# Centroid products of the later pairs moved in front of the odd cycles' products with v

## The chip, the cores and the metric

The kernel runs on one core of one Trainium2 chip. The metric is the device time of one execution in microseconds (us). The kernel before takes 772.41 us (median of three runs, 772.18 to 772.73). About 0.2% (1.5 us) is what a measurement of this kernel can tell from no change.

## The reference, cut to what matters

Clustered attention (2 batches, 8 heads, 768 rows, head width 64, 16 centroids per head) is followed by two dense blocks on 1536 x 512 tokens. The dense blocks are not touched.

```
q_assign = argmax(q_n @ c_n.T)          # nearest centroid of each query row
k_assign = argmax(k_n @ c_n.T)          # nearest centroid of each key row
scores = where(q_assign == k_assign, q @ k.T / 8, -1e9)
attn = exp(scores - max) / (sum + 1e-9)
out = attn @ v
x = out (heads side by side); x = moe(x); return moe2(x)
```

## The kernel before, in words

The attention works on 8 pairs (batch, two heads) numbered 0 to 7. A pair's queries and keys are turned by TensorE, split into a high and a low part (`th`, `tl`), and stacked by DMAs on SP's queue into two tiles per head, `st` for queries and `st` for keys; one-hot rows of the assigned centroids are stacked under them, so that one product gives scores and mask.

**Cycles.** The scores of one head are 12 blocks of 128 rows, worked off in two halves of 6. There are 16 heads, so 16 *cycles* d = 0 to 15. In a cycle, `run_cycle` reads a string of words, left to right, and each word issues its instructions on all engines; every engine runs its own instructions in exactly that order (the kernel is in a manual schedule). The words:

- `S5` to `S10`: the scores of a block (four matmuls, lines 582 and 585, into one of two `s` buffers of PSUM), then on VectorE the negated row maximum `nm` (line 591). Blocks are numbered from the cycle's own first; S6 to S10 belong to the next cycle.
- `E5` to `E10`: on ScalarE the exponential of a block into `p` with its row sum (line 600). It also frees the `s` buffer: S9 uses that of S7, and so waits for E7.
- `T0` to `T11`, `t0` to `t11`: three transposes of `p` blocks by TensorE into one of three `pt` buffers of PSUM (line 637; the same three buffers serve every preparatory transpose and product named below), and the copy to SBUF, by ScalarE for `T` (line 642), by VectorE for `t` (line 640). The fourth in a row waits until the first is copied out.
- `V`: the product of the cycle's transposed blocks with v (line 651), 24 matmul records of tiles 64 columns wide.
- `P`: the next step of preparing a later pair. A pair has 12 steps: `q0`, `q1`, `k0`, `k1` (turn a half of the queries or keys, line 497, ScalarE's copy at line 503, GpSimd's split at lines 479 and 480; `k1` also loads a later pair); `dt` (the products with the centroids, line 518, 8 matmul records of tiles 32 columns wide, then ScalarE's copy `dc`, line 521); `pd` (`dc` turned back, line 525); `max/ge` (VectorE, lines 534 and 535); a multiplication on GpSimd (line 537); `stack0` (five DMAs of head 0, line 475); a maximum (line 543); a comparison (line 545); `po` (load of the next v, three transposes at line 553, ScalarE's `oht` at line 555, four DMAs of one-hot rows of head 0).
- `K`: the stacking of the pair's second head, first the five DMAs, at the second K its four one-hot DMAs.
- `R`: the reciprocal of the row sums on VectorE, GpSimd's `line`, a DMA `flat`. `B`: its spreading back by two DMAs. `X`, `Y`: the scaled result and its split. `W`, `w`: one step of a weight conversion, most of them on VectorE.

Pair i is prepared from the end of cycle 2i-4 to the middle of cycle 2i-2; its first scores are S6 of cycle 2i-1. Cycle 0 has a string of its own (BEGIN), cycles 1 to 12 use ODD and EVEN in turn, and cycles 13 to 15 have strings of their own. Pair 1's `dt` stands in the opening part, those of pairs 2 to 7 in ODD.

```
scores_of(n): scores(n, 0); scores(n, 1); row_max(n)
"P": next(made, None)
"K": second.pop(0)(1)
```

Of the kernel before, what the change touches and what calls it, by code (L numbers as in the profile page):

```python
# [19 lines left out]
P = 128  # L20
# [13 lines left out]
def attention_moe_moe(  # L34
# [19 lines left out]
    B, H, S, D = q.shape  # L54
# [150 lines left out]
    with ExitStack() as actx:  # L205
# [483 lines left out]
        def run_cycle(d, order):  # L689


            for word in order.split():
                what, arg = word[0], int(word[1:] or 0)
                n = NJ * d + arg
                if what == "S":
                    if n < NJ * NDBL:
                        scores_of(n)
                elif what == "E":
                    if n < NJ * NDBL:
                        row_exp(n)  # L700
                elif what in "Tt":
                    p_transpose(2 * d + arg // NJ, arg % NJ, what == "t")
                    next_slot()
                elif what == "P":
                    next(made, None)
                elif what == "R":
                    inverse(d)
                elif what == "V":
                    p_v(d)
                elif what == "X":  # L710
                    if opsum:
                        x_rows(min(opsum))
                elif what == "K":
                    if second:
                        second.pop(0)(1)
                elif what == "B":
                    spread()
                elif what == "Y":
                    if x32s:
                        x_parts()  # L720
                elif what in "Ww":
                    pump(1 if d >= FIRST + (what == "w") else 0)
                elif what == "N":
                    next_slot()
            if d == 3:
                issue_chunk(0)

        PRE = ""
        BEGIN = "S3 P T0 T1 S4 E3 P T2 E4 P T3 S5 E5 t4 T5 S6 T6 T7 E6 P R S7 t8 T9 E7 T10 P B S8 P E8 P K S9 K P t11 S10 V E9 E10"
        EVEN = "P S5 T0 T1 P t2 E5 S6 T3 P T4 E6 t5 S7 R T6 P T7 E7 K S8 X T8 T9 E8 Y t10 B K S9 P w P E9 t11 S10 W E10 V"  # L730
        ODD = "S5 T0 T1 P t2 S6 E5 T3 T4 t5 S7 E6 P T6 R E7 T7 X S8 Y P E8 t8 T9 S9 T10 B P t11 E9 W S10 V P P E10 W"
        LATE_ODD = "S5 T0 T1 t2 E5 S6 T3 R T4 t5 S7 X Y E6 T6 T7 E7 S8 E8 t8 T9 S9 T10 B t11 S10 E9 V W W W E10"
        LATE_EVEN = "S5 T0 t1 t2 E5 S6 T3 T4 E6 R T5 S7 X Y E7 T6 S8 T7 t8 W S9 E8 t9 B T10 E9 t11 W S10 W V E10"
        LAST = "S5 T0 E5 t1 T2 T3 X t4 R t5 Y t6 T7 t8 B T9 t10 T11 W V W W W X Y"
# [1 line left out]
        for d in range(-1, NDBL):  # L736
            run_cycle(d, PRE if d < 0 else BEGIN if d == 0 else
                      {13: LATE_ODD, 14: LATE_EVEN, 15: LAST}.get(d, (EVEN, ODD)[d % 2]))
        manual.close()
# [145 lines left out]
```

## Time and profile before

| | |
|---|---|
| median of the runs | 772.41 us |
| profiled execution, its own time | 772.37 us |
| its span (first to last instruction) | 770.6 us |
| TensorE busy | 761.0 us (99%) |
| VectorE, ScalarE, GpSimd busy | 568.6, 360.9, 255.0 us |
| attention, with cycles 0 to 15 | about the first 245 us |

The span is the time on the core; the execution's own time has 1.8 us around it. In the profile PE is TensorE's matmul, DVE is VectorE, ACT ScalarE, POOL GpSimd, SPq the DMA queue of SyncE. A matmul's end is modelled, so PE counts as busy over small gaps; the starts tell more.

### The profile page before, as it was taken

The page shows a single profiled execution, that of the slowest core. Times are in us where ns is not written, and L with a number is a line of the kernel's source. Part 1 is how long each engine was busy: PE and PEld are TensorE (multiplying, and loading weights), DVE is VectorE, ACT ScalarE, POOL GpSimd, SP SyncE. Part 2 cuts the span into 40 slices and gives each one's busy share as a digit, 9 for nine tenths or more (in the row PEclk, how much of TensorE's full clock was granted, in tenths as well). Part 3 has the DMA queues.
Part 4 walks back from the last instruction along what each step waited for, and adds up shares of the span by engine and source line. Part 5 has one row for each costly group of instructions (what it writes and reads, how often), then busy time and mean ns, then how long its engine had stood idle before and what let it go on. Part 6 is the DMA issues. An engine that isn't in the chain of part 4 may idle for free.

```text
span 770.6 us, 10609 instructions
## 1 busy us (share of the span) xinstructions
PE 761.0 (99%) x3888; PEld 606.6 (79%) x3889; DVE 568.6 (74%) x824; ACT 360.9 (47%) x672; POOL 255.0 (33%) x390
## 2 busy tenths in 40 slices
PE   8999999999999999999999999999999999999998
PEld 5677777777776888888888888888888888888886
DVE  6676588797888868787798787888867787555552
ACT  6777676777574544534334343333534222222220
POOL 6347458566544412222221133422222211111110
PEclk9999999999999999999999999999999999999999
DMA  8865767665532123113131121021121111000012
GB/s 203 213 156 132 196 144 189 154 172 131 132 99 68 54 108 100 64 56 110 54 110 56 55 98 67 4 106 56 55 105 60 54 56 56 0 1 1 27 42 95
DMA packets 49667, 70.10 MB, mean 91 GB/s; under 512 B 28592, under 2 KB 33936, under 8 KB 49616
## 3 DMA queue, kind: packets, MB, share of 16 engines
q1 hardware_dynamic: 49328, 69.27, 31.6%
q8 instruction: 30, 0.49, 0.3%
q10 hardware_dynamic: 288, 0.16, 0.1%
q14 instruction: 21, 0.17, 0.1%
HBM read 46.17 MB, written 3.19 MB: 64 GB/s over the span
## 4 chain that ended last, share of the span: by engine, by line
PE 84%; DVE 4%; DMA 4%; ACT 3%; POOL 2%; issue 1%; SPq 1%; DVEq 0%; ACTq 0%; POOLq 0%
PE h L790 11%; PE h L788 11%; PE y L790 11%; PE h L789 11%; PE y L789 11%; PE y L788 11%; PE o L651 6%; PE pt L637 3%; PE s L582 3%; PE s L585 2%; ACT p L600 2%; DVE nm L591 2%; DMA st<-tl 1%; ACT p_t L642 1%; DMA st<-t 1%
## 5 line engine op out<-in xcount | busy, mean ns | idle before, releaser
L750 POOL TENSOR_SCALAR gh<-g 128x512 fp32r<-128x512 f32 x96 | 71.1, 741 | 290.1 <-DVE g L781 165.0
L788 PE MATMUL h<-xh,w 128*128 128x512 f32 x384 | 149.5, 389 | 0.2 <-ACT p L600 0.2
L790 PE MATMUL h<-xh,w 128*128 128x512 f32 x384 | 149.6, 390 | 0.0
L789 PE MATMUL h<-xl,w 128*128 128x512 f32 x384 | 149.5, 389 | 0.0
L591 DVE TENSOR_REDUCE nm<-s 128x1 f32<-128x768 f32 x96 | 91.5, 953 | 42.2 <-PE s L585 39.8
L600 ACT ACTIVATE p<-s,nm 128x768 f32<-128x768 f32 x96 | 87.5, 911 | 20.3 <-DVE nm L591 19.0
L777 ACT ACTIVATE p<-h,ones 128x512 f32<-128x512 f32 x48 | 33.0, 689 | 134.1 <-DVE m L776 133.7
L754 DVE TENSOR_TENSOR gl<-g,gh 128x512 fp32r<-128x512 f32 x96 | 72.1, 751 | 22.3 <-POOL gh L750 16.1
L790 PEld LDWEIGHTS h<-xh,w 128*128 128x128 f32 x384 | 72.1, 188 | 15.5 <-issue 0.6
L788 PEld LDWEIGHTS h<-xh,w 128*128 128x128 f32 x384 | 72.1, 188 | 15.2 <-issue 0.4
L789 PEld LDWEIGHTS h<-xl,w 128*128 128x128 f32 x384 | 72.1, 188 | 15.0
L637 PE MATMUL pt<-ident,p 128*128 128x128 f32 x576 | 81.2, 274 | 1.5 <-ACT p L600 0.6
L642 ACT ACTIVATE p_t<-pt 128x384 f32<-128x384 f32 x126 | 57.4, 491 | 40.8 <-PE pt L637 39.9
L582 PE MATMUL s<-st,st 128*128 128x384 f32 x192 | 73.7, 384 | 2.1 <-ACT p L600 0.8
L637 PEld LDWEIGHTS pt<-ident,p 128*128 128x128 f32 x576 | 66.9, 140 | 11.2 <-ACT p L600 4.9
L788 PE MATMUL y<-gh,w 128*128 128x512 f32 x192 | 74.7, 389 | 0.0
L789 PE MATMUL y<-gl,w 128*128 128x512 f32 x192 | 74.7, 389 | 0.0
L790 PE MATMUL y<-gh,w 128*128 128x512 f32 x192 | 74.7, 389 | 0.0
L788 PE MATMUL y<-w,gh 128*128 128x512 f32 x192 | 74.7, 389 | 0.0
L789 PE MATMUL y<-w,gh 128*128 128x512 f32 x192 | 74.7, 389 | 0.0
L790 PE MATMUL y<-w,gl 128*128 128x512 f32 x192 | 74.7, 389 | 0.0
L154 ACT ACTIVATE wx<-wraw 128x1024 f32<-128x1024 f32 x32 | 36.5, 1140 | 80.2 <-DVE w L173 32.0
(122 smaller groups left out, 1320.6 us busy)
## 6 DMA issues: line engine op xcount, KB each, us to landing
wraw<-in_moe_w_in_dram SPq DMA_DIRECT2D x16, 1024.0 KB
wraw<-in_moe_w_out_dram SPq DMA_DIRECT2D x16, 1024.0 KB, 4.6
st<-t SPq DMA_DIRECT2D x24, 192.0 KB, 4.1
st<-th SPq DMA_DIRECT2D x10, 384.0 KB, 3.8
st<-th SPq DMA_DIRECT2D x20, 192.0 KB, 4.3
st<-tl SPq DMA_DIRECT2D x19, 192.0 KB
nat<-in_q_dram SPq DMA_DIRECT2D x8, 384.0 KB, 3.7
nat<-in_k_dram SPq DMA_DIRECT2D x8, 384.0 KB, 5.1
```

Source lines behind the costliest of these rows:

```text
L154: nc.scalar.activation(x, high.bitcast(F32), AF.Abs)
L582: nc.tensor.matmul(s[:, step, :HS], qt[:, 0, cols], kt[:, 0, kc], start=True, stop=False)
L591: nc.vector.tensor_reduce(nm, s[:, :, :HS], AX.XY, ALU.max, negate=True)
L600: nc.scalar.activation(p, s[:, :, :HS], AF.Exp, bias=nm, accum_out=dens[d][:, jj:jj + 1])
L637: nc.tensor.transpose(ps[:, jj * P:(jj + 1) * P], p[:, kt * P:(kt + 1) * P], ident)
L642: nc.scalar.activation(pt, ps, AF.Copy)
L651: nc.tensor.matmul(o[hf * D:(hf + 1) * D], prepped[i][0][:, h, kt], pts.pop((2 * d + hf, kt)), start=kt == 0, stop=kt == NJ - 1)
L750: nc.gpsimd.tensor_scalar(hi, g, 1.0, 0.0, ALU.mult, ALU.add)
L754: nc.vector.tensor_tensor(lo, g, hi.bitcast(F32), ALU.subtract)
L788: nc.tensor.matmul(o, lh, rh, start=first, stop=False)
L789: nc.tensor.matmul(o, lh, rl, start=False, stop=False)
L790: nc.tensor.matmul(o, ll, rh, start=False, stop=last)
```

## The change

Two of the strings are written anew; nothing else changes. The number of each kind of word in a pair of cycles stays the same, but two copies per odd cycle go from ScalarE to VectorE (t9 and t10 were T9 and T10).

```
-EVEN = "P S5 T0 T1 P t2 E5 S6 T3 P T4 E6 t5 S7 R T6 P T7 E7 K S8 X T8 T9 E8 Y t10 B K S9 P w P E9 t11 S10 W E10 V"
-ODD = "S5 T0 T1 P t2 S6 E5 T3 T4 t5 S7 E6 P T6 R E7 T7 X S8 Y P E8 t8 T9 S9 T10 B P t11 E9 W S10 V P P E10 W"
+EVEN = "T0 P S5 T1 t2 E5 S6 P T3 T4 R T5 E6 T6 P T7 K S7 P E7 S8 X Y T8 t9 E8 t10 B K S9 P E9 t11 w S10 P E10 W V"
+ODD = "P S5 T0 T1 t2 S6 E5 T3 T4 t5 S7 E6 P T6 R S8 E7 T7 X Y E8 t8 t9 S9 t10 B t11 E9 W S10 P V W P P P E10"
```

In ODD the six P are, before: `k0`, `k1`, `dt`, `pd`, `max/ge`, the GpSimd multiplication. After, in the same order: `k0` in front of S5, `k1`, `dt` directly in front of V, and `pd`, `max/ge` and the multiplication behind V. In EVEN they are `stack0`, the maximum, the comparison, `po`, and `q0`, `q1` of the next pair.

On TensorE in an odd cycle (d = 5, pair 4) this stood at the centroid products before:

```order
L582 MATMUL s38_1521<-st1_3_0_958,st0_3_0_957 128x384
L585 MATMUL s38_1521<-st1_3_0_958,st0_3_0_957 128x384
L518 MATMUL dt4_1534<-t32_4_0_0_1370,cn32_67 32x384
L518 MATMUL dt4_1534<-t32_4_1_0_1437,cn32_67 32x384
L518 MATMUL dt4_1534<-t32_4_0_1_1378,cn32_67 32x384
L518 MATMUL dt4_1534<-t32_4_1_1_1488,cn32_67 32x384
L637 MATMUL pt11_2_1543<-ident_60,p33_1382 128x128
L637 MATMUL pt11_2_1543<-ident_60,p34_1399 128x128
```

and this stands there now (o5 is the product with v of this cycle):

```order
L582 MATMUL s40_1572<-st1_3_0_958,st0_3_0_957 128x384
L585 MATMUL s40_1572<-st1_3_0_958,st0_3_0_957 128x384
L518 MATMUL dt4_1580<-t32_4_0_0_1370,cn32_67 32x384
L518 MATMUL dt4_1580<-t32_4_1_0_1418,cn32_67 32x384
L518 MATMUL dt4_1580<-t32_4_0_1_1393,cn32_67 32x384
L518 MATMUL dt4_1580<-t32_4_1_1_1488,cn32_67 32x384
L651 MATMUL o5_1587<-p10_t0_1433,v32_2_520 64x384
L651 MATMUL o5_1587<-p11_t0_1499,v32_2_520 64x384
```

The products moved from between a score block and a transpose to between the last score block and V.

On ScalarE, in the even cycle behind it (d = 6), from E5 (p41) to E7 (p43) stood before:

```order
L600 ACTIVATE p41_1643,den6_1481<-s41_1617,nm41_1622 128x768
L642 ACTIVATE p12_t3_1656<-pt12_3_1652 128x384
L642 ACTIVATE p12_t4_1663<-pt12_4_1659 128x384
L600 ACTIVATE p42_1666,den7_1665<-s42_1645,nm42_1650 128x768
L642 ACTIVATE p13_t0_1696<-pt13_0_1692 128x384
L555 ACTIVATE oht4_1704<-po4_1700,ohbias_63,ohscale_62 128x384
L642 ACTIVATE p13_t1_1714<-pt13_1_1710 128x384
L600 ACTIVATE p43_1716,den7_1665<-s43_1674,nm43_1679 128x768
```

and now (p12_t5 is the copy of T5, which VectorE made before):

```order
L600 ACTIVATE p41_1642,den6_1481<-s41_1623,nm41_1628 128x768
L642 ACTIVATE p12_t3_1656<-pt12_3_1652 128x384
L642 ACTIVATE p12_t4_1662<-pt12_4_1658 128x384
L642 ACTIVATE p12_t5_1679<-pt12_5_1675 128x384
L600 ACTIVATE p42_1682,den7_1681<-s42_1644,nm42_1649 128x768
L642 ACTIVATE p13_t0_1688<-pt13_0_1684 128x384
L642 ACTIVATE p13_t1_1695<-pt13_1_1691 128x384
L555 ACTIVATE oht4_1715<-po4_1711,ohbias_63,ohscale_62 128x384
L600 ACTIVATE p43_1721,den7_1681<-s43_1702,nm43_1707 128x768
```

One copy more stands between the two exponentials.

On SP's queue in an even cycle (d = 10, pair 6; flat is R's DMA, st..._0 are head 0's tiles, st..._1 head 1's) stood before:

```order
L616 DMA flat10_2517<-line10_2512 6x128
L241 DMA v32_7_2525<-in_v_dram 128x2x384
L475 DMA st0_6_0_2186<-oht6_2531 16x384 x2
L475 DMA st1_6_0_2187<-oht6_2531 16x384 x2
L475 DMA st0_6_1_2188<-th6_2184 64x2x768
L475 DMA st0_6_1_2188<-tl6_2185 64x768
L475 DMA st1_6_1_2189<-th6_2184 64x768 x2
L475 DMA st1_6_1_2189<-tl6_2185 64x768
```

and now:

```order
L616 DMA flat10_2500<-line10_2495 6x128
L475 DMA st0_6_1_2188<-th6_2184 64x2x768
L475 DMA st0_6_1_2188<-tl6_2185 64x768
L475 DMA st1_6_1_2189<-th6_2184 64x768 x2
L475 DMA st1_6_1_2189<-tl6_2185 64x768
L241 DMA v32_7_2536<-in_v_dram 128x2x384
L475 DMA st0_6_0_2186<-oht6_2542 16x384 x2
L475 DMA st1_6_0_2187<-oht6_2542 16x384 x2
```

Head 1's five stacking DMAs moved in front of the load of v and head 0's one-hot rows.

## Rows read from the trace of the kernel before

**Rows 1.** The page's first part: busy time, share of span, instructions.

```profile
PE 761.0 (99%) x3888; PEld 606.6 (79%) x3889; DVE 568.6 (74%) x824; ACT 360.9 (47%) x672; POOL 255.0 (33%) x390
```

**Rows 2.** Timeline of PE: V of cycles 6, 7, 9, 10, 11, 12 (start us, us).

```profile
118.21 4.09 PE L651 MATMUL o<-p_t,v 128*64 128x384 f32 x24
133.14 4.09 PE L651 MATMUL o<-p_t,v 128*64 128x384 f32 x24
161.44 4.09 PE L651 MATMUL o<-p_t,v 128*64 128x384 f32 x24
175.17 4.09 PE L651 MATMUL o<-p_t,v 128*64 128x384 f32 x24
189.74 4.09 PE L651 MATMUL o<-p_t,v 128*64 128x384 f32 x24
204.31 4.09 PE L651 MATMUL o<-p_t,v 128*64 128x384 f32 x24
```

**Rows 3.** Timeline of PE, even cycle 10: S5, last run of transposes before S9, S9.

```profile
165.46 0.44 PE L582 MATMUL s<-st,st 128*128 128x384 f32 x1
...
171.35 1.15 PE L637 MATMUL pt<-ident,p 128*128 128x128 f32 x9
172.56 0.44 PE L582 MATMUL s<-st,st 128*128 128x384 f32 x1
```

**Rows 4.** Timeline of PE, odd cycle 11.

```profile
180.67 0.49 PE L497 MATMUL ptq<-ident,nat 128*128 128x128 f32 x3
181.14 0.55 PE L637 MATMUL pt<-ident,p 128*128 128x128 f32 x3
...
185.47 0.34 PE L585 MATMUL s<-st,st 80*128 80x384 f32 x1
185.74 0.85 PE L518 MATMUL dt<-t,cn 128*32 128x384 f32 x8
186.52 0.88 PE L637 MATMUL pt<-ident,p 128*128 128x128 f32 x6
187.15 0.42 PE L582 MATMUL s<-st,st 128*128 128x384 f32 x1
...
187.94 0.49 PE L637 MATMUL pt<-ident,p 128*128 128x128 f32 x3
188.27 0.49 PE L525 MATMUL pd<-ident,dc 128*128 128x128 f32 x3
...
188.86 0.42 PE L582 MATMUL s<-st,st 128*128 128x384 f32 x1
```

**Rows 5.** Timeline of PE in the opening part: pair 1's dt and what follows.

```profile
16.59 0.85 PE L518 MATMUL dt<-t,cn 128*32 128x384 f32 x8
17.38 0.84 PE L411 MATMUL po<-ident,dots 128*64 128x128 f32 x6
```

**Rows 6.** Timeline of ACT, even cycle 10: copies of T0 and T1, E5, E7.

```profile
166.86 0.87 ACT L642 ACTIVATE p_t<-pt 128x384 f32<-128x384 f32 x2 [2.16 <-PE pt L637]
167.62 0.90 ACT L600 ACTIVATE p<-s,nm 128x768 f32<-128x768 f32 x1
...
171.50 0.92 ACT L600 ACTIVATE p<-s,nm 128x768 f32<-128x768 f32 x1
```

**Rows 7.** Timeline of DVE at the end of cycle 9 and start of 10.

```profile
163.53 0.54 DVE L534 TENSOR_REDUCE mx<-pd 128x24 f32<-128x384 f32 x1
164.18 0.56 DVE L535 TENSOR_TENSOR eq<-pd,mx 128x384 f32<-128x384 f32 x1
...
166.47 0.96 DVE L591 TENSOR_REDUCE nm<-s 128x1 f32<-128x768 f32 x1 [0.60 <-PE s L585]
```

**Rows 8.** Timeline of SP's queue, even cycle 8: R's flat, head 1's five DMAs.

```profile
144.40 0.29 SPq L616 DMA_DIRECT2D flat<-line  x1
...
147.85 5.22 SPq L475 DMA_DIRECT2D st<-t  x5
```

**Rows 9.** DMA issues of 144.7 to 147.8 us: KB each, median us to landing.

```profile
st<-oht SPq DMA_DIRECT2D x4, 24.0 KB, 3.0
```

## The prediction

> **What bounds the kernel now.** The page's first part comes first: TensorE is busy 99% of the span [rows 1], so on the face of it only what TensorE is spared can shorten anything. That share hides small waits, because a matmul's modelled end covers them, so I read TensorE's timeline by starts. The distance from one V to the next gives the length of a cycle: even cycle 10 takes 13.73 us, odd cycle 11 14.57 us; cycle 7 takes 14.93 and cycle 12 14.57, both longer than their kind [rows 2]. V lasts 4.02 us (161.44 to 165.46) [rows 2, 3], so the rest of the cycle is 9.71 us in the even one and 10.55 in the odd one.
>
> Unit prices on TensorE [rows 4]: a score block behind a transpose 0.79 us (187.15 to 187.94), a T or any other three transposes 0.33 (187.94 to 188.27), two that end a run 0.59 (188.27 to 188.86), so the last of a run 0.26. With these the hidden waits show. In even cycle 10 the run of three before S9 takes 1.21 us (171.35 to 172.56) instead of 0.92: S9 needs the buffer that E7 frees, and E7 started 1.06 us before S9 [rows 3, 6]. In odd cycle 11 the word behind k0 starts 0.47 after it instead of 0.33 [rows 4], since it reuses T0's buffer. So the loop is bound by TensorE and ScalarE together: outside V the score blocks go no faster than the exponentials free their buffers. What decides here is how ScalarE's list falls in with TensorE's.
>
> **The odd cycle.** The move takes dt (0.78, 185.74 to 186.52) out of the middle, with 0.09 in front of it (0.27 from the block's last matmul, under 0.2 between a block's own) and 0.04 behind it (two T take 0.63 instead of 0.59) [rows 4]. In front of V it costs 0.78 again; the 0.09 was paid there already. How a 32-wide product passes into a 64-wide one is shown by pair 1: 0.79 from dt to the 64-wide transposes [rows 5], the same as into full-width ones. So the move itself is worth 0.13 us a pair. Bounds: if the passage into V were free, another 0.13 less; if V paid its 0.09 again, 0.09 more. I take 0.13, since rows 5 are the same kind of passage.
>
> The Trainium skill, TensorEngine Tiling (Array Packing), section Key Properties, says that changing the tiling mode, and not just the tile, drains TensorE. By that rule 32-wide to 64-wide is a change like any other, one of a pair's four changes goes, and the gain is one passage; rows 5 agree. Read the other way, that neighbours which are both column-tiled need no drain, the whole would come out 6 x 0.13 = 0.8 us lower.
>
> Now the walk from V's end to the next V, in the prices above, with waits: k0 and S5 1.04; T0, T1, t2 and S6 1.70; T3, T4, t5 and S7 1.70; k1 and T6 0.58; a wait of 0.13, since S8 needs E6, which ScalarE starts at 4.11 and which frees its buffer 1.06 later, at 5.17, where TensorE comes at 5.04; S8 0.79; T7, t8, t9 0.92; S9 0.79 (E7 frees it just in time, at 6.87); t10 and t11 0.58, with 0.10 because t11 reuses t8's buffer and VectorE has that copy only behind X; S10 0.88 with the change of mode; dt 0.78. Sum 9.99, against 10.55: minus 0.55 a cycle, of which pd's 0.33 is only moved. The two copies given to VectorE are covered: it finishes t11's copy after S10, while V still has 4 us to go. The W steps around V run in those 4 us as well; without that cover each would push nm10 or the max/ge step, but E10 is wanted only in the next cycle's S6.
>
> **The even cycle.** It now opens with pd and T0 (0.59) in front of S5; pd waits for nothing, as ScalarE copies dc during V. Behind pd VectorE must do max/ge before nm5, since it is issued first. A copy out of PSUM starts 0.59 after its transposes (166.86 is 1.40 behind S5's start, of which the block itself takes 0.8) [rows 3, 6], so the maximum starts at 0.58, the comparison 0.65 later (163.53 to 164.18) and is out of nm5's way about 0.5 after that [rows 7], at 1.70. The scan of S5 could start at 0.59 plus 1.0 (165.46 to 166.47) [rows 3, 7], so it loses 0.1 and ends at 2.66; E5 starts 0.1 later, 2.76 (in the rows 0.19 behind the scan, 167.43 to 167.62, with ScalarE still at its copies, so this is the most [rows 6, 7]). Before, max/ge was done during V and E5 started 2.16 after V's end [rows 3, 6].
>
> From E5 to E7 ScalarE needed 3.88 us (167.62 to 171.50): two exponentials, four copies out of PSUM, one of them oht. Now one copy of 0.38 (two in 0.76, 166.86 to 167.62) stands there more [rows 6]: 4.26. E7 starts at 7.02, S9 at 8.08. TensorE by itself would come there at 0.59 + 0.79 + 0.59 + 0.79 + 1.58 (T3 to T7) + 0.79 + 0.26 (po) + 0.79 + 0.92 = 7.10. So TensorE waits about 1.0 us before S9 in all, part of it earlier, at T6, which reuses the buffer of T3, whose copy is queued behind E5. Behind S9: 0.79, q0 and t11 0.59, S10 0.79, q1 0.33 and the change of mode 0.09, V at 10.67 against 9.71: plus 0.95. E8 ends in time for S10. The GpSimd multiplication starts behind max/ge and is wanted by VectorE only behind nm6, some 2 us later; each us beyond that would come on top.
>
> **SP's queue.** Head 0's one-hot rows are now issued behind head 1's five DMAs. Before, flat went out 7.24 after V's end (144.40 against 133.14 + 4.02) [rows 2, 8]. R stands earlier now; I take 6.2 (bounds 5.5 and 7.24). Flat, v and the one-hot rows took 3.45 to issue, the five DMAs 5.22 [rows 8]; issue of the last one-hot rows begins at about 6.2 + 3.45 + 5.22 - 0.6 = 14.3 and lands 3.0 later [rows 9], at 17.3. S6 of the next odd cycle wants them 14.7 + 2.2 = 16.9 after. That is 0.4 late, with every term at the size of this one cycle. I add 0.6 us once, for a cycle with a weight load in the queue; the bounds are 0 and about 1 us in each of six cycles.
>
> **Sum.** Six odd cycles -3.3; cycle 7's excess of 0.36 over its kind goes, -0.4; five even ones (2 to 10) +4.8; cycle 12, which has no q0 and q1 and now V at 10.27, 14.29 against 14.57, -0.3; DMA +0.6. Together +1.4: span 770.6 + 1.4 = 772.0, execution 772.37 + 1.4 = 773.8. The profiled execution lies 0.04 below the median 772.41, so the same figure stands for a median.
>
> **Rivals.** *The even cycle's wait does not grow.* If E7 is no later against TensorE than before, the wait stays 0.3, S9 comes at 7.4, the even cycle costs +0.3, cycle 12 gains 0.9: -3.3 - 0.4 + 1.5 - 0.9 = -3.1, 769.2 us. For it: two copies leave ScalarE in the odd cycle, and ScalarE is busy 47% [rows 1]. Against it: those copies leave the other cycle, and the even one has one more in just the stretch that decides.
>
> *The one-hot rows come late in every odd cycle.* Place: S6 of cycles 3 to 13, TensorE standing behind a DMA. It decides from a landing 16.9 us after the odd V's end. If the rows come at 17.7, 0.8 x 6 = 4.8 instead of 0.6: 778.0 us, slower. For it: nine DMAs in one queue and 5.22 us for five issues [rows 8]. Against: it needs the size of cycle 8's terms, or more, in each of the six; a landing 0.4 faster hides it all.
>
> *The move saves no passage.* Then 0.13 x 6 = 0.8 is missing: 774.6, within the forecast's own range.
>
> **Chances.** Forecast 0.60 (own range 772.0 to 775.6, from 0.15 a cycle on 12 cycles), the first rival 0.17, the late DMA 0.20, something else 0.03. A change of under 0.2% (772.41 +- 1.5) can't be told from none. Faster: 0.14, nearly all from the first rival. Slower by over 0.2%, from 773.95: not quite half of the forecast (0.27) and the late DMA, 0.47. Same: 0.39. The range 770.8 to 777.0 leaves out the outer half of both rivals.
>
> **What would show it.** In the new trace: dt to V 0.78 to 0.79; odd cycles of about 14.0, even ones of about 14.7; E7 7.0 after the odd V's end and S9 1.06 after E7; no wait of TensorE on a DMA. Even cycles of 14.0 show the first rival; gaps between t2 and S6 in the odd cycles, with one-hot DMAs landing at that time, the second. The forecast falls if S9 does not follow E7.

## The result, and the profile after

The changed kernel takes 779.11 us (median of five runs, 777.50 to 780.62) beside 772.46 (772.18 to 773.02) for the kernel before on the same chip: a ratio of 1.0082, 95% interval 1.0070 to 1.0094. It is slower by 0.8%. The forecast was 773.8 with a range up to 777.0, so the result lies above it; the value of the rival *the one-hot rows come late in every odd cycle*, 778.0, came nearest. The profiled run took 779.11 us, its span is 777.3 against 770.6.

First the page, its first part; it answers to [rows 1]:

```profile
PE 764.1 (98%) x3889; PEld 608.2 (78%) x3889; DVE 573.9 (74%) x836; ACT 358.1 (46%) x660; POOL 254.0 (33%) x390
```

TensorE is busy 3.1 us longer and idle 3.6 us longer, and its work is the same. Twelve copies went from ScalarE to VectorE, the net of the two strings.

Then the list of waits, for TensorE, its longest line (engine, tile and line, releaser: us in total, times, longest us):

```profile
PE s L585 <- DMA st<-oht: 3.0, 3, 2.6
```

This line is new: the second matmul of a score block waits for the one-hot rows, the thing that the prediction said would not be seen. Where, the timeline of TensorE tells (start us, us, line, operation, tiles, count, idle time in front and its releaser). V of cycles 6, 7, 9, 10, 11 and 12 answer to [rows 2]:

```profile
104.93 0.85 PE L518 MATMUL dt<-t,cn 128*32 128x384 f32 x8
105.71 4.09 PE L651 MATMUL o<-p_t,v 128*64 128x384 f32 x24
...
117.71 0.44 PE L582 MATMUL s<-st,st 128*128 128x384 f32 x1 [0.17 <-ACT p L600]
120.32 4.09 PE L651 MATMUL o<-p_t,v 128*64 128x384 f32 x24
...
134.95 4.09 PE L651 MATMUL o<-p_t,v 128*64 128x384 f32 x24
...
156.23 0.41 PE L585 MATMUL s<-st,st 80*128 80x384 f32 x1 [0.22 <-DMA st<-oht]
164.15 4.09 PE L651 MATMUL o<-p_t,v 128*64 128x384 f32 x24
...
178.76 4.09 PE L651 MATMUL o<-p_t,v 128*64 128x384 f32 x24
...
184.78 0.42 PE L582 MATMUL s<-st,st 128*128 128x384 f32 x1
187.77 0.66 PE L585 MATMUL s<-st,st 80*128 80x384 f32 x1 [2.57 <-DMA st<-oht]
...
188.87 2.12 PE L637 MATMUL pt<-ident,p 128*128 128x128 f32 x9
...
191.08 0.34 PE L585 MATMUL s<-st,st 80*128 80x384 f32 x1
...
197.19 4.09 PE L651 MATMUL o<-p_t,v 128*64 128x384 f32 x24
...
211.34 4.09 PE L651 MATMUL o<-p_t,v 128*64 128x384 f32 x24
```

dt now stands in front of V, 0.78 us (104.93 to 105.71), as forecast. Cycle 11 takes 18.43 us (178.76 to 197.19) instead of 14.57. In it TensorE stands 2.57 us behind the one-hot rows, and what follows is slow: from S6's second matmul to S7's second, 3.31 us (187.77 to 191.08). The view of busy times by stretch shows why (stretch, its length, then for PE, PEld, DVE, ACT and POOL the busy us and count, the granted clock, the share of the DMA engines, GB/s):

```profile
178.76:185.00 6.24, 6.24 (x42) 3.75 (x41) 2.89 (x3) 4.04 (x9) 2.39 (x3) 1.00 1.02 227
185.00:187.00 2.00, 0.20 (x2) 0.00 (x0) 0.59 (x2) 1.22 (x3) 0.85 (x2) 1.00 0.24 67
187.00:189.00 2.00, 1.23 (x4) 1.16 (x5) 0.00 (x0) 0.00 (x0) 1.92 (x3) 0.66 0.38 96
189.00:191.00 2.00, 2.00 (x11) 2.00 (x10) 0.96 (x1) 1.11 (x3) 1.69 (x3) 0.50 0.09 23
191.00:193.00 2.00, 2.00 (x15) 1.93 (x15) 1.70 (x4) 1.61 (x5) 0.27 (x1) 0.99 0.00 0
```

After the wait the granted clock is 0.50, TensorE's lower level (1.2 of 2.4 GHz), and back at 0.99 from 191 on.

The lengths of the cycles, each worked out from two starts of V as in the fence above (us; the names of the experiments are those of the next section):

| cycle | 1 | 2 | 3 | 4 | 5 | 6 | 7 | 8 | 9 | 10 | 11 | 12 |
|---|---|---|---|---|---|---|---|---|---|---|---|---|
| before | 14.56 | 13.74 | 14.55 | 13.76 | 14.55 | 13.73 | 14.93 | 13.73 | 14.57 | 13.73 | 14.57 | 14.57 |
| after | 14.29 | 14.60 | 14.58 | 14.61 | 14.49 | 14.61 | 14.63 | 14.61 | 14.59 | 14.61 | 18.43 | 14.15 |
| rows first | 14.26 | 14.60 | 14.12 | 14.61 | 14.11 | 14.60 | 14.56 | 14.61 | 14.13 | 14.60 | 14.60 | 14.18 |
| rows last | 14.79 | 13.74 | 15.87 | 13.73 | 18.65 | 13.73 | 16.21 | 13.73 | 16.01 | 13.73 | 19.91 | 13.69 |
| odd only | 14.41 | 14.83 | 14.12 | 14.83 | 14.12 | 14.84 | 14.53 | 14.83 | 14.12 | 14.87 | 14.16 | 14.86 |
| even only | 14.76 | 14.19 | 14.75 | 14.19 | 15.16 | 14.19 | 14.94 | 14.18 | 14.62 | 14.18 | 18.02 | 13.75 |
| v behind | 14.14 | 14.62 | 14.14 | 14.60 | 14.14 | 14.60 | 14.54 | 14.62 | 14.13 | 14.61 | 15.66 | 14.17 |
| k0 and t7 | 15.17 | 13.59 | 14.30 | 13.61 | 14.29 | 13.60 | 14.48 | 13.60 | 14.31 | 13.61 | 15.10 | 14.38 |

Of the 6.7 us that the span grew, 4.3 are the five even cycles 2 to 10 (0.87 each), 3.9 is cycle 11 alone; the other odd cycles gave 0.6 back, cycle 12 0.4, and the opening part and cycle 13 0.5.

Why the rows are late: SP's issues, of cycle 6 and of cycle 10 (start us, us for the group, DMA, count):

```profile
116.09 0.26 SPq L616 DMA_DIRECT2D flat<-line  x1
...
121.84 2.81 SPq L475 DMA_DIRECT2D st<-oht  x4
...
168.21 0.40 SPq L144 DMA_DIRECT2D wraw<-in_moe_w_out_dram  x1
...
174.52 0.26 SPq L616 DMA_DIRECT2D flat<-line  x1
...
175.92 1.66 SPq L475 DMA_DIRECT2D st<-tl  x1
...
180.54 0.40 SPq L241 DMA_DIRECT2D v<-in_v_dram  x1
181.48 2.87 SPq L475 DMA_DIRECT2D st<-oht  x4
```

From flat to the end of the one-hot issues it is 8.56 us in cycle 6 and 9.83 in cycle 10. And the same two cycles by stretches of 4 us, the last two columns (DMA share, GB/s):

```profile
113.57:117.57 4.00, 3.78 (x27) 3.21 (x26) 3.48 (x9) 4.00 (x11) 1.05 (x4) 1.00 0.15 34
...
172.00:176.00 4.00, 3.77 (x27) 3.21 (x26) 3.47 (x9) 4.00 (x11) 1.05 (x4) 1.00 1.05 269
176.00:180.00 4.00, 3.86 (x25) 3.00 (x27) 4.00 (x7) 3.22 (x9) 3.15 (x4) 1.00 1.04 229
180.00:184.00 4.00, 4.00 (x27) 2.18 (x24) 0.73 (x1) 2.53 (x4) 1.23 (x2) 1.00 1.04 236
```

In cycle 6 the DMA engines have an idle stretch before head 1's stacking starts. In cycle 10 a weight load (`wraw`) went out at 168.21, and they are full for 12 us on end. The one-hot rows, last in the queue, land at about 187.7.

### The profile page after: what moved, and what is told of

Its sections match the earlier page's. It is cut to its first block, busy times and chain, and to the rows that moved or that the text cites. A ratio compares the mean times of both kernels' runs of the same rounds, so it can differ in the third digit from the quotient of the medians.

```text
span 777.3 us, 10579 instructions
## 1 busy us (share of the span) xinstructions
PE 764.1 (98%) x3889; PEld 608.2 (78%) x3889; DVE 573.9 (74%) x836; ACT 358.1 (46%) x660; POOL 254.0 (33%) x390
## 4 chain that ended last, share of the span: by engine, by line
PE 86%; DVE 4%; ACT 3%; DMA 3%; SPq 2%; issue 1%; DVEq 0%; ACTq 0%
PE h L790 11%; PE h L788 11%; PE y L790 11%; PE h L789 11%; PE y L788 11%; PE y L789 11%; PE o L651 6%; PE pt L637 4%; PE s L582 3%; PE s L585 3%; ACT p L600 2%; DVE nm L591 2%; SPq L475 1%; DMA st<-oht 1%; ACT p_t L642 1%
## 5 line engine op out<-in xcount | busy, mean ns | idle before, releaser
L754 DVE TENSOR_TENSOR gl<-g,gh 128x512 fp32r<-128x512 f32 x96 | 73.7, 768 | 22.3 <-POOL gh L750 16.3
L790 PEld LDWEIGHTS h<-xh,w 128*128 128x128 f32 x384 | 72.1, 188 | 15.5 <-issue 0.6
L834 DVE TENSOR_TENSOR acc<-y,acc 128x512 f32<-128x512 f32 x71 | 48.3, 684 | 32.1 <-PE y L790 32.1
```

The costliest lines, as they stand in the source:

```text
L754: nc.vector.tensor_tensor(lo, g, hi.bitcast(F32), ALU.subtract)
L790: nc.tensor.matmul(o, ll, rh, start=False, stop=last)
L834: nc.vector.tensor_tensor(a, po, a, ALU.add)
```

## The experiments

The ratios are to the kernel before, run on the same chip in the same hour (772.97, 773.11 or 773.2 us there). Theory: the time was lost to the order on SP's queue, and in the even cycle to ScalarE's list. Rivals: the move saves nothing, or the even cycle loses it elsewhere.

**Rows first.** The changed kernel with K (head 1's stacking) put behind the P that follows S7 (`po`), so that head 0's one-hot rows stand in front of head 1's stacking again.

```
-EVEN = "... T6 P T7 K S7 P E7 S8 ..."
+EVEN = "... T6 P T7 S7 P K E7 S8 ..."
```

> The changed kernel, with head 1's five stacking DMAs (first K of EVEN) issued behind the load of v and head 0's one-hot rows again, as before the change; nothing moves on another engine. Theory A (the order on SP's queue makes the one-hot rows late): TensorE's waits on the one-hot DMA go (0.2 to 0.4 us in cycles 3, 5 and 9, 2.6 us in cycle 11, and the low clock behind it), cycle 11 falls from 18.4 to about 14.3 us, even cycles stay at 14.6: 779.1 - 4.7 = 774.4, up to 0.8 more if cycle 12 gets back its stall of before. Rival B (the queue is simply full in cycle 10, with a weight load of 1 MB, whatever the order): cycle 11 stays at 17 to 18 us, 778 to 779.

Measured: 774.37, ratio 1.0018 (1.0009 to 1.0027). No wait for `st<-oht` is left, and cycle 11 is 14.60. The span is 772.1: 5.2 us below that of the changed kernel. Even cycles stay at 14.60. Its timeline of TensorE in cycle 11, from S6's second matmul to V:

```profile
183.56 0.34 PE L585 MATMUL s<-st,st 80*128 80x384 f32 x1
...
185.25 0.34 PE L585 MATMUL s<-st,st 80*128 80x384 f32 x1
...
189.89 0.55 PE L637 MATMUL pt<-ident,p 128*128 128x128 f32 x3 [0.39 <-DVE p_t L640]
```

S6's second matmul to S7's second is 1.69 here (183.56 to 185.25), against the 3.31 above: the lower clock cost 1.62 us in cycle 11, beside the 2.57 of waiting; together 4.19.

**Rows last.** The opposite, on the kernel before: only K is moved ahead of `po`.

```
-EVEN = "... S7 R T6 P T7 E7 K S8 ..."
+EVEN = "... S7 R T6 K P T7 E7 S8 ..."
```

> The kernel before, with only the opposite done: its first K put in front of the po step, so that head 1's five DMAs are issued ahead of v and head 0's one-hot rows. Theory A: the order alone costs, as in the changed kernel, 0.2 to 0.4 us in some odd cycles and 3 to 4 us in cycle 11 with the low clock: 776 to 777. If the lateness needs the rest of the change too, 772.4 to 773.5. Since R's flat goes out 1 us later here and even cycles are 0.9 us shorter, the rows would rather be later than in the changed kernel, which speaks for 777 or more.

Measured: 782.11, ratio 1.0127 (1.0103 to 1.0152), well above the 776 to 777 expected. The order alone makes the kernel before 9 us slower. (The profiled run took 785.88; the lengths of its cycles in the table are those of that run.) Of its waits and its timeline of TensorE, cycles 5 and 11:

```profile
PE s L585 <- DMA st<-oht: 9.9, 6, 3.6
```

```profile
100.15 0.42 PE L585 MATMUL s<-st,st 80*128 80x384 f32 x1 [2.27 <-DMA st<-oht]
...
193.54 0.66 PE L585 MATMUL s<-st,st 80*128 80x384 f32 x1 [3.61 <-DMA st<-oht]
```

Every odd cycle from the third on waits. The even cycles keep their 13.73: the even cycle's loss has nothing to do with this order.

**Odd only.** The new ODD with the old EVEN.

```
-EVEN = "T0 P S5 T1 t2 E5 S6 P T3 T4 R T5 ..."
+EVEN = "P S5 T0 T1 P t2 E5 S6 T3 P T4 E6 t5 ..."
```

> The new ODD string with the old EVEN string. The DMA order is the old one, so no wait on one-hot rows. Theory A with my walk: odd cycles about 14.1 us (14.56 before), even cycles: pd and max/ge still stand in front of the scan of S5, E5 starts about 0.6 later than before, ScalarE's list has its old length, so S9 0.6 later: 14.3. Sum 6 x (-0.45) + 5 x 0.6 = about 0.3 more, minus the odd excess of cycle 7: 772.4 give or take 1.0. Rival (the even cycle's loss comes from ScalarE's extra copy alone): even cycles 13.8 to 14.0 with pd's 0.33, total 770.5.

Measured: 775.93, ratio 1.0040 (1.0026 to 1.0054): a miss. Odd cycles came to 14.12, but the even ones to 14.84, +1.1. From VectorE's timeline (V ends at 109.28):

```profile
109.87 0.56 DVE L534 TENSOR_REDUCE mx<-pd 128x24 f32<-128x384 f32 x1 [1.64 <-PE pd L525]
...
111.00 0.95 DVE L591 TENSOR_REDUCE nm<-s 128x1 f32<-128x768 f32 x1
```

max/ge stands in front of S5's scan, which starts 1.72 after V's end (1.01 in [rows 3, 7]). The old string is no better home for a pd that stands behind V.

**Even only.** The old ODD with the new EVEN.

```
-ODD = "P S5 T0 ... S10 P V W P P P E10"
+ODD = "S5 T0 T1 P t2 ... S10 V P P E10 W"
```

> The new EVEN string with the old ODD string. pd and max/ge are done in the odd cycle again. DMA order is the new one. Theory A: even cycles S9 about 0.5 later than before (one copy more on ScalarE, E5 hardly later): 14.2; odd cycles 14.56 plus the waits on one-hot rows, about 4.5 in all: 772.4 + 5 x 0.5 + 4.5 = 779.4. If pd's place, and not the copy, makes the even cycle longer: 13.8 and 777.

Measured: 776.67, ratio 1.0048 (1.0033 to 1.0062). Even cycles take 14.19, 0.46 more than before, the size foretold; of these, 0.12 is E5's later start (2.28 after V's end instead of 2.16) and 0.30 the longer way from E5 to E7 (4.18 instead of 3.88). The time came below the 779.4 expected, in part because cycle 12 is 0.82 shorter than before, which that sum left out. The wait for `st<-oht` is there (2.0 us in two), and cycle 11 takes 18.02. From its timeline of TensorE in cycle 11:

```profile
186.53 0.41 PE L585 MATMUL s<-st,st 80*128 80x384 f32 x1 [1.65 <-DMA st<-oht]
...
188.87 0.67 PE L582 MATMUL s<-st,st 128*128 128x384 f32 x1
```

The matmul behind this wait still takes 0.41, but S7's first takes 0.67: the lower clock came here too, behind a wait of 1.65, and only some 2 us after it.

**dt apart.** Rows first, with dt one word earlier, so that it is not V's neighbour.

```
-ODD = "... E9 W S10 P V W ..."
+ODD = "... E9 W P S10 V W ..."
```

> As e1_rows_first, but dt stands in front of S10 instead of behind it, so a score block lies between the centroid products and V; the rest is the same. If the neighbourhood of dt and V saves one change of tile width (0.13 us in the prediction's sum), odd cycles grow from 14.12 to 14.25 and the whole by 0.8 us against e1. If a passage between column tiles is free, they grow by 0.26, 1.6 us. If the neighbourhood saves nothing, they stay at 14.1.

Measured: 775.41, ratio 1.0029 (1.0019 to 1.0039); odd cycles 14.33 against 14.12. Its timeline of TensorE, cycle 5:

```profile
102.51 0.99 PE L637 MATMUL pt<-ident,p 128*128 128x128 f32 x6
103.44 0.85 PE L518 MATMUL dt<-t,cn 128*32 128x384 f32 x8
104.22 0.44 PE L582 MATMUL s<-st,st 128*128 128x384 f32 x1
...
105.12 4.09 PE L651 MATMUL o<-p_t,v 128*64 128x384 f32 x24
```

The two transposes before dt take 0.93 here (102.51 to 103.44). In *rows first* the same two, before S10, take 0.75. To be V's neighbour is worth 0.2 us a pair: the rival without any saving falls. The 0.2 lies between 0.13 and twice that, so the sum alone doesn't tell one passage from two. What tells is dt itself: it takes 0.78 to the next instruction in front of a score block (103.44 to 104.22), and 0.78 in front of V in the changed kernel (104.93 to 105.71). So the passage from dt into V is no cheaper than one into full width. The Trainium skill, TensorEngine Tiling (Array Packing), section Key Properties, says that a change of tiling mode drains TensorE; by it the passage from dt into V is a change like any other, one in a pair is saved and not two, and the trace agrees (0.78 in both places).

**t5 on VectorE.** Rows first, with the copy of T5 given back to VectorE and R behind it.

```
-EVEN = "... T3 T4 R T5 E6 T6 P T7 ..."
+EVEN = "... T3 T4 t5 E6 T6 P R T7 ..."
```

> As e1_rows_first, but T5's copy in EVEN is VectorE's again (t5, with R behind the comparison), so ScalarE has one copy less between E5 and E7. If the even cycle's length comes from ScalarE's list alone, E7 comes 0.38 earlier and even cycles fall from 14.6 to 14.2, the whole by 2.3 us. By the walk with all waits they fall by 0.1 only: T6 still waits for T3's copy behind E5, S7 stands behind T6 and T7, and the scan of S7 ends at 6.85 behind V's end, so E7 starts at 6.95 instead of 7.0.

Measured: 773.17, ratio 0.9999 (0.9990 to 1.0009): level with the kernel before. Even cycles fell to 14.48, by 0.12. ScalarE's timeline, E5, E6 and E7 of cycle 6 (V ends at 108.69):

```profile
111.39 0.90 ACT L600 ACTIVATE p<-s,nm 128x768 f32<-128x768 f32 x1 [0.21 <-DVE nm L591]
...
113.03 0.91 ACT L600 ACTIVATE p<-s,nm 128x768 f32<-128x768 f32 x1
...
115.51 0.90 ACT L600 ACTIVATE p<-s,nm 128x768 f32<-128x768 f32 x1
```

E6 starts 1.64 behind E5 instead of 2.00, but E7 stands 6.82 after V's end, 0.06 earlier than in the changed kernel. With one copy less in ScalarE's list, two other things end just in front of E7, `oht` on ScalarE (115.50) and VectorE's scan of S7 (the scan behind it starts at 115.54); which of them decides isn't shown.

**Weight load later.** The changed kernel with the loads for the weight conversion one step later, so that none stands in front of cycle 10's stacking.

```
-FIRST = 4
+FIRST = 5
```

> The changed kernel, with the weight conversions begun one cycle later (FIRST 5), so that the 1 MB weight load which stands in the queue at the start of cycle 10 is issued at that cycle's end. If the long wait of cycle 11 (2.6 us on the one-hot rows, and the low clock behind it) needs both the new order and the weight load, it shrinks to the 0.2 to 0.4 us of the other odd cycles, cycle 11 to 14.6, and the low clock is gone: about 775.3, if the later weights cost nothing behind cycle 15. If the order alone does it, cycle 11 stays at 18 and the time at 779.

Measured: 785.12, ratio 1.0152 (1.0139 to 1.0166). The total missed the 775.3 expected; for the rows in cycle 11 it is an answer. Its waits of TensorE, and the weight load in SP's timeline:

```profile
PE s L582 <- ACT p L600: 5.4, 10, 3.4
PE h L788 <- DVE g L767: 1.7, 1, 1.7
...
PE s L585 <- DMA st<-oht: 1.1, 2, 0.7
```

```profile
188.05 0.53 SPq L144 DMA_DIRECT2D wraw<-in_moe_w_out_dram  x1
```

The load goes out at 188.05, not at 168.21, and cycle 11's wait for the rows is gone with the order unchanged. The two waits left are in cycles 5 and 9 (0.67 and 0.39). Cycle 11 still takes 15.99 and not the 14.6 expected: a transpose waits 1.23 us behind VectorE's copy, which stands behind a step of the weight conversion. And weights that come later are converted later: cycle 14 grew to 18.40 us (13.12 in the changed kernel), with a 3.4 us wait behind E and slow matmuls after it, and the part behind the cycles is 2 us longer.

**One-hot rows on ScalarE's and on GpSimd's queue.** The changed kernel with head 0's four one-hot DMAs issued by another engine.

```
-copy(dst, oht[r0:r0 + C])
+copy(dst, oht[r0:r0 + C], nc.gpsimd if h == 0 else None)   # the other: nc.scalar
```

> The changed kernel with head 0's four one-hot DMAs issued by GpSimd instead of SP. GpSimd has nothing to do at that point in cycle 10 (idle 181.3 to 186.1 us). Theory (place in SP's queue): waits for st<-oht gone, cycle 11 at 14.6, the whole 774.5 (774 to 775.5). Rival (full DMA engines): cycle 11 keeps a wait above 1.5 us, 777 to 779.

Measured: 775.12, ratio 1.0026 (1.0016 to 1.0036), and no wait for the rows; cycle 11 takes 14.30. Its GpSimd timeline, and its busy times around that (V ends at 167.79):

```profile
175.13 2.00 POOL L475 DMA_DIRECT2D st<-oht  x4 [1.01 <-ACT oht L555]
```

```profile
171.79:175.79 4.00, 3.70 (x27) 3.23 (x27) 3.48 (x8) 4.00 (x11) 1.71 (x6) 1.00 1.04 258
```

The rows go out 7.3 us after V's end, 6.35 us earlier than in the changed kernel (175.13 against 181.48), into DMA engines that are as full as there (share 1.04), and are in time. So it is the place in SP's queue, behind head 1's stacking and v, that made them late; full DMA engines alone did not. They do cost: the four rows take 7.7 us to land here (median), against 3.0 in [rows 9]. The span is 1.1 us above that of *rows first*; cycle 2 is 0.86 longer here, with a wait of 0.64 us behind a ScalarE copy.

> The changed kernel with head 0's four one-hot DMAs issued on ScalarE's queue, right behind oht, instead of SP's. Theory (place in SP's queue decides): the rows no longer stand behind the five stacking DMAs and v; TensorE's waits for st<-oht (3.0 us, the longest 2.6) are gone, odd cycles come to 14.1 (7 and 11 14.6). Rival (the 16 DMA engines are full from 172 to 184 us, whatever queue a transfer comes from): the wait of cycle 11 stays above 1.5 us. Beside it a price: the four issues stand between oht and E7 on ScalarE. At nothing the even cycles stay 14.6 and the whole comes to about 774.5; at SP's 0.7 us for each (2.87 for four) E7 and S9 are 2.8 us later in each of six cycles, about 790.

Measured: 813.16, ratio 1.0511 (1.0492 to 1.0529). The rows are in time here too (cycle 11 takes 14.06), but ScalarE pays for the issues, and more than was allowed for. In its list of waits of TensorE:

```profile
PE s L582 <- ACT p L600: 27.7, 10, 4.7
```

The even cycles 2 to 10 take 19.4 to 21.1 us, 4.8 to 6.5 more than in *rows first*. The four issues keep ScalarE for 2.45 to 4.33 us (97.05 to 101.38 in cycle 4); 2.87 was allowed. The other 1.6 to 2.4 us had no place in that sum: matmuls are slow behind the waits (a score block's first takes up to 0.69), at a granted clock of 0.978 on average over the run.

**v behind.** The changed kernel with the next v loaded behind head 0's one-hot rows.

```
-if i < len(pairs) - 1: load_v(i + 1)      # ahead of po
 one_hots(0)
+if i < len(pairs) - 1: load_v(i + 1)
```

> The changed kernel with the load of the next v issued behind head 0's one-hot DMAs instead of in front of them; the five stacking DMAs stay in front. Theory (what stands in front in the queue counts by its issue time and its bytes): the rows go out 0.9 us earlier (180.54 instead of 181.48) and land 0.9 to 1.7 us earlier (384 KB at the 230 GB/s of that stretch), so the waits of cycles 3, 5 and 9 go and that of cycle 11 falls from 2.6 to 0.9 to 1.7 us. If TensorE's clock then stays up, another 1.6 us go: 774.9 to 777.5 in all, 776 in the middle. If only the five stacking DMAs count, no change: 779.

Measured: 774.63, ratio 1.0013 (1.0004 to 1.0023), just below the range expected. The only wait for the rows left is this one in cycle 11 (from TensorE's timeline):

```profile
184.81 0.41 PE L585 MATMUL s<-st,st 80*128 80x384 f32 x1 [0.98 <-DMA st<-oht]
```

No score matmul behind it in cycle 11 takes more than 0.45, and the run's granted clock is 1.000: the clock stayed up. With one DMA of 384 KB per even cycle out of the rows' way, 4.1 us of span came back, of the 5.2 that the order cost.

**k0 and t7.** The kernel before with two small moves: k0 to the front of ODD, and in EVEN T7's copy on VectorE (`t7`) with R behind it.

```
-ODD = "S5 T0 T1 P t2 S6 ..."       EVEN = "... S7 R T6 P T7 E7 K S8 ..."
+ODD = "P S5 T0 T1 t2 S6 ..."       EVEN = "... S7 T6 P t7 R E7 K S8 ..."
```

> A version meant to beat both: the kernel before with two things learnt from the walk. k0 goes in front of S5 in ODD, as in the changed kernel, which ends t2's wait on T0's copy (0.2 us a cycle); in EVEN T7's copy goes to VectorE in front of R, so that E7 starts 0.38 earlier and S9's wait of 0.31 goes. Odd cycles 14.36, even ones 13.4 to 13.6: 6 x 0.2 + 6 x 0.2 to 0.3 = 2.4 to 3 us less than before, 769.5 to 770. If VectorE's list becomes the limit in the even cycle, only the odd part stays: 771.2.

Measured: 770.60, ratio 0.9967 (0.9954 to 0.9979): faster than both kernels, and 2.5 us below the kernel before, within the 2.4 to 3 expected. Odd cycles take 14.30, even ones 13.60; in cycle 1 a one-hot wait of 0.57 appears, and cycles 1 and 11 (15.17 and 15.10) are longer than before.

## Why the prediction was wrong, step by step

**The step that failed is "SP's queue".** It said: "That is 0.4 late, with every term at the size of this one cycle. I add 0.6 us once, for a cycle with a weight load in the queue; the bounds are 0 and about 1 us in each of six cycles." The order costs 5.2 us of span instead of 0.6 (changed kernel against *rows first*), and reversed on the kernel before 9 us (*rows last*). The mechanism had been named, by the rival too; its price was wrong, in three ways.

First, the sum left out what the walk had found. A lateness of 0.4 at the size of an ordinary cycle is 0.4 in each ordinary cycle; the sum had 0.6 for one cycle and nothing for the others, without a reason. In cycles 3, 5 and 9 the late rows cost 0.46, 0.38 and 0.46 (changed kernel against *rows first*; the timeline shows a wait of 0.2 in two of them), in cycle 7 0.07. So here the walk itself held: in cycle 6 the four issues end at 124.65 and take 0.7 each, so the last begins 14.2 after V's end at 109.73, forecast 14.3.

Second, the terms were read off one ordinary cycle, [rows 8], and the cycle that decides was the one with the most in the queue. In cycle 10, with a weight load ahead, the last issue begins at 183.65, 15.5 after 168.17, and the matmul that needs the rows starts 4.1 later, where [rows 9] have 3.0: 19.6 in place of 17.3. That is a wait of 2.57, not 0.4 or 0.6. The weight load is one half of the reason (*weight load later* takes this wait away), the place in the queue the other (*rows first* and *GpSimd's queue* take it away with the load still in front). A load in an even cycle is not enough by itself: in cycle 4 one went out at 78.03, 2.6 us before V's end (80.63), and cycle 5 lost only 0.38. What makes that difference wasn't tested.

Third, the price stopped at the wait. After it TensorE ran at the lower clock for some 3 us, another 1.62. In the changed kernel's five runs the clock granted on average goes with the time: 1.000 in the run of 777.50 us, 0.995 in that of 780.62.

Three cycles at 0.4, cycle 7 at 0.1 and cycle 11 at 3.8 come in sum to 5.2, about what the rival priced at 0.8 in each of six (4.8). So its 778.0 came near by luck: the rows were not that late in every odd cycle. The range's upper end, 777.0, lay below this value, although the rival had a chance of 0.20.

**The odd cycle** was right but for size: 14.12 without late rows, forecast 14.02. Step by step in *rows first* the walk is off by no more than 0.07 anywhere. Two odd cycles, 7 and 11, are 0.45 longer than their kind, with a transpose behind VectorE's copy (0.39 in cycle 11); the prediction let cycle 7's excess vanish. So odd cycles gave 1.95 us in place of 3.7. In these two cycles VectorE's first step of R (128 x 6 numbers, line 607) takes 0.44 and 0.66 us, in all others 0.16, and both times it ends 0.03 after a GpSimd instruction that it overlaps (at 129.60 and 187.53, against 129.57 and 187.50). That VectorE stood behind GpSimd there is read from these times and wasn't tested.

**The even cycle** was right, and it was the term forecast to decide. ScalarE's timeline in cycle 6 of the changed kernel, where V ends at 109.73:

```profile
112.44 0.90 ACT L600 ACTIVATE p<-s,nm 128x768 f32<-128x768 f32 x1 [0.20 <-DVE nm L591]
...
116.61 0.95 ACT L600 ACTIVATE p<-s,nm 128x768 f32<-128x768 f32 x1
```

E5 starts at 2.71 (forecast 2.76), E7 at 6.88 (7.02), S9 at 117.71, 7.98 (8.08), 1.10 behind E7, where [rows 3, 6] have 1.06. Even cycles came to 14.61, forecast 14.68. Before, E7 stood 6.04 after V's end in this cycle. Of the 0.84 more, 0.55 is E5's later start (2.71 instead of 2.16) and 0.29 the longer way from E5 to E7 (4.17 instead of 3.88). *Even only* takes the sum apart: the new EVEN string costs 0.46 with the old ODD, and pd and max/ge behind V 0.42 more with the new one. With the old EVEN they cost 1.1 (*odd only*), so the parts don't simply add up. The rival *the even cycle's wait does not grow* falls. The copy's length is not its worth: given back to VectorE, a copy of 0.38 shortened the even cycle by 0.12 (*t5 on VectorE*).

**The move itself** saves a passage: 0.2 a pair, forecast 0.13 with bounds of 0.04 and 0.26. Cycle 12 came to 14.15, forecast 14.29.

The sum without late rows: *rows first* lies 1.5 us of span above the kernel before, and the forecast without its 0.6 was +0.8. It is made of odd cycles 1.75 too good, even ones 0.5 too dear and 0.5 at the opening part and cycle 13 not foreseen. So without the queue the kernel is slower by a little, as forecast, though the odd cycles gave little more than half of their term.

## What to carry to other kernels

When a change moves DMAs past each other, walk the queue in the cycle that has the most in it (a weight load, a reload of v), not in an ordinary one, and price what waits behind it with the slow matmuls that follow. Small rows that a near product needs belong in front of large transfers that nobody waits for yet; here that order alone was worth 5 to 9 us. A product put next to one of its kind saves one passage, 0.2 us a pair here; what the move brought with it, one copy more on ScalarE and max/ge in front of a scan, cost 0.87 us in each even cycle.

## What was not expected of the hardware

Waits of 2.57 us (changed kernel), 1.65 (*even only*), and 2.27 and 3.61 (*rows last*) were each followed by the lower clock, at a cost of 1.62 us behind the first of them; one of 0.98 (*v behind*) was not. The matmul right behind a wait doesn't tell: it took 0.41 in *even only* and 0.42 behind the 2.27, and the slow ones came some 2 us later.

What one issue costs SP varies: in cycle 10 of the changed kernel one stacking DMA took 1.66 us, and all five 4.91 (175.23 to 180.14), against 4.35 in its cycle 6 and 5.22 in [rows 8]. Four one-hot DMAs issued by GpSimd took it 2.00 to 2.17 us, issued by ScalarE 2.45 to 4.33.
